# Attention and a two-layer network on one core: how Q, K and V are brought on chip

## The chip, the cores and the metric

The kernel runs on one core of a Trainium2 chip. The time is the device time of one execution in microseconds (us), lower is better. Inputs and outputs lie in the chip's memory (DRAM) as 32-bit floats; the kernel computes in bf16 with 32-bit accumulation.

## The reference, cut to what matters

```python
# q, k, v: [8 batches, 8 heads, 576 rows, 64]; beacon_k, beacon_v: [8, 8, 16, 64]
k_all = concatenate([beacon_k, k], axis=2)
v_all = concatenate([beacon_v, v], axis=2)
scores = q @ k_all.T / 8            # causal mask on the 576 own rows, beacons always seen
a = softmax(scores)
x = (a @ v_all)                     # to [4608 tokens, 512]
h = x @ w_in                        # w_in [512, 2048]
out = maximum(0.01 * h, h) @ w_out  # w_out [2048, 512]
```

## The kernel before

The attention is done in 32 steps `g`, one for each pair of heads: `g = 4 * b + hp` for batch `b` and pair `hp`. A step of the main loop does several things at once, one step apart from each other:

- `t_q(g+1, 0)` and `t_q(g+1, 1)` turn the next pair's queries and keys by TensorE (PE) transposes into `qT` and `kT`, with a copy out of PSUM by VectorE (DVE). Each takes six transposes, since the 576 rows of a head lie as 96 partitions with six rows each (`RI = 6`, `RP = 96`). The 16 beacon columns of `kT` are two small copies by GpSimd (POOL).
- `score(g, 0..3)` multiplies keys by queries; ScalarE (ACT) takes the exponential of each part into `aT`. `masks(g)` zeroes the causal triangle on DVE.
- `value(g-1, 0)` and `value(g-1, 1)` multiply `aT` by `v_aug`, whose 65th column of ones yields the row sums; DVE divides. `x_transposes(g-1)` brings the result into `xT`.
- `fill(m, n)` with `m = g - 5` puts pieces of the two-layer network (`moe1`, `moe2`) between these. So no piece of the network runs before step 5, and `w_out` is first needed in step 9. After step 32 only network pieces are left.

The order of the instructions on each engine is that of the code; nothing reorders them. Queries and keys come as plain 32-bit transfers on SyncE's queue (SP), in runs of 1536 bytes, and are cast to bf16 by POOL (the first few by DVE). Values come by POOL's own queue, whose transfers cast on the way, straight into `v_aug`; their runs in DRAM are one row, 256 bytes. The weights come by POOL's queue too, in eight transfers of 1 MB read each, runs of 2048 bytes, two of them issued in each of the first steps. POOL therefore casts queries and keys, copies beacon columns and issues transfers, all in one line.

A transfer that POOL issues takes one of eight counters in turn (`DMASW0` to `DMASW7` in the order below), so it is issued only when the transfer eight before it has landed. SP and ACT have eight of their own (`DMAHW0` to `DMAHW7`).

Of the kernel before, what the change touches and what calls it, by code (L numbers as in the profile page):

```python
# [8 lines left out]
FP32 = mybir.dt.float32  # L9
BF16 = mybir.dt.bfloat16  # L10
# [5 lines left out]
def kernel(  # L16
# [11 lines left out]
    nc = tc.nc  # L28
# [12 lines left out]
    RI = 6  # L41
    RP = S // RI

# [25 lines left out]
    natpool = ctx.enter_context(tc.tile_pool(name="natpool", bufs=2))  # L69
# [29 lines left out]
    bkT = singles.tile([128, B, H, NB], BF16, name="bkT")  # L99
# [17 lines left out]
    def load_qk(b, h0, nh, q_eng, k_eng):  # L117

        if b not in nat:
            nat[b] = (  # L120
                natpool.tile([RP, RI, H, D], BF16, name="q_nat"),
                natpool.tile([RP, RI, H, D], BF16, name="k_nat"),
            )
        hs = slice(h0, h0 + nh)
        for src, dst, name, eng in ((q, nat[b][0], "q_raw", q_eng), (k, nat[b][1], "k_raw", k_eng)):
            raw = rawpool.tile([RP, 4, RI, D], FP32, name=name)
            nc.sync.dma_start(
                out=raw[:, 0:nh],
                in_=src[b, hs].rearrange("h (p i) d -> p h i d", i=RI),
            )  # L130
            eng.tensor_copy(  # L131
                out=dst[:, :, hs, :],
                in_=raw[:, 0:nh].rearrange("p h i d -> p i h d"),
            )
# [4 lines left out]
    def load_beacon_k():  # L139
        nc.scalar.dma_start(out=bk_raw, in_=beacon_k.rearrange("b h n d -> (h n) b d"))  # L140
        nc.gpsimd.tensor_copy(
            out=bk, in_=bk_raw[:, :, None, :].to_broadcast([128, B, 2, D])
        )

    def beacon_transposes(b0, b1):

        ps = ps_one.tile([128, 1024], BF16, name="tp", tag="one")
        for b in range(b0, b1):
            nc.tensor.transpose(
                ps[:, b * 128 : (b + 1) * 128], bk[:, b].rearrange("p e d -> p (e d)"), ident  # L150
            )
        nc.vector.tensor_copy(
            out=bkT[:, b0:b1].rearrange("p b h n -> p (b h n)"), in_=ps[:, b0 * 128 : b1 * 128]
        )

    def load_v(b):
        t = v_bufs[b % 2]
        nc.gpsimd.dma_start(
            out=t[0:NB, 0, :, 0:D], in_=beacon_v[b].rearrange("h p d -> p h d")
        )  # L160
        nc.gpsimd.dma_start(
            out=t[NB:128, 0, :, 0:D], in_=v[b, :, 0:112].rearrange("h p d -> p h d")
        )
        for c in (1, 2, 3):
            nc.gpsimd.dma_start(  # L165
                out=t[:, c, :, 0:D],
                in_=v[b, :, OFF[c] : OFF[c] + 128].rearrange("h p d -> p h d"),
            )
        nc.gpsimd.dma_start(
            out=t[0:80, 4, :, 0:D], in_=v[b, :, 496:576].rearrange("h p d -> p h d")  # L170
        )
# [3 lines left out]
    def t_q(g, which):  # L175

        b, hp = divmod(g, NPAIR)
        hs = slice(2 * hp, 2 * hp + 2)
        if which == 0:
            dst = headpool.tile([128, S], BF16, name="qT")  # L180
            qk[g] = [dst]
        else:
            kT = headpool.tile([128, NB + S], BF16, name="kT")
            for par in range(2):
                ps_ = slice(par * 64, par * 64 + 64)
                nc.gpsimd.tensor_copy(out=kT[ps_, 0:NB], in_=bkT[ps_, b, 2 * hp + par, :])  # L186
            qk[g].append(kT)
            dst = kT[:, NB : NB + S]
        ps = ps_one.tile([128, 1024], BF16, name="tp", tag="one")
        for i in range(RI):  # L190
            nc.tensor.transpose(  # L191
                ps[:, i * RP : (i + 1) * RP],
                nat[b][which][:, i, hs, :].rearrange("p h d -> p (h d)"),
                ident[0:RP, 0:RP],
            )
# [161 lines left out]
    def has(g):  # L357
        return 0 <= g < NG
# [10 lines left out]
    with order:  # L369
        load_qk(0, 0, 2, nc.vector, nc.vector)  # L370
        load_beacon_k()
        load_qk(0, 2, 2, nc.vector, nc.gpsimd)
        load_v(0)
        load_qk(0, 4, 4, nc.gpsimd, nc.gpsimd)
        weights = [(load_w_in, i) for i in range(4)] + [(load_w_out, i) for i in range(4)]
        for f, i in weights[:2]:
            f(i)
        weights = weights[2:]
        beacon_transposes(0, 1)
        t_q(0, 0)  # L380
        t_q(0, 1)
        beacon_transposes(1, B)

        for g in range(NG + 1):
            b, hp = divmod(g, NPAIR)
            m = g - NPAIR - 1
            if b + 1 < B:
# [6 lines left out]
            for f, i in weights[:2]:  # L394
                f(i)
            weights = weights[2:]
# [59 lines left out]
```

## Time and profile before

| | us |
|---|---|
| median of 3 runs (lowest, highest) | 399.04 (398.98, 399.43) |
| the profiled execution | 399.55 |
| its span in the trace | 397.9 |
| PE busy in the span | 353.9 (89%) |
| ACT, DVE, POOL busy | 191.2, 168.7, 103.5 |
| bytes that the transfers wrote | 38.09 MB |

The span runs from the first to the last instruction of the trace; the 1.65 us between it and the profiled execution's time lie around it. A busy PE is not always a PE at its peak, since its instructions overlap. The transfers are counted by the bytes written, so one that casts from 32 to 16 bits counts half of what it reads. A "packet" is one run, counted on the engine that moves it; 16 transfer engines share the work, and their shares can add up to more than 1 since packets overlap. Queue q0 is POOL's, q1 is SP's, and q10 is ACT's, which brings `bk_raw` alone (1024 runs of 256 bytes, without a cast).

### The profile page before, as it was taken

Reading aid. Unit: us, or ns where it says so; the run is one execution under the profiler, and the core shown is the slowest. Engines: PE = TensorE matmul, PEld = TensorE weight load, DVE = VectorE, ACT = ScalarE, POOL = GpSimd, SP = SyncE. Lnnn points to the kernel's source line nnn. Section 1 sums busy time; section 2 is a strip of 40 time slices with the busy share of each in tenths; the row PEclk is TensorE's granted clock in tenths of the full one; section 3 lists DMA queues with packets and bytes.
Section 4 is the critical chain, followed back from the end, with each engine's and each line's share of the span. In section 5 each row is a group of like instructions: output and inputs, shape, how many; then the busy total and the mean of one; then the engine's idle time right before and its main releaser. Section 6 shows DMA issues by size and latency. Waiting matters only on the chain.

```text
span 397.9 us, 7236 instructions
## 1 busy us (share of the span) xinstructions
PE 353.9 (89%) x2997; PEld 185.0 (47%) x3048; DVE 168.7 (42%) x362; ACT 191.2 (48%) x305; POOL 103.5 (26%) x161
## 2 busy tenths in 40 slices
PE   2167068999999999999999999999999999999996
PEld 2035035565555555545555555555555454444442
DVE  3146036775445644565455445544444320101021
ACT  1063037786555555555555555555555633333300
POOL 3973375335002270237023602260000000000000
PEclk9999999999999999999999999999999999999999
DMA  8999999909005590559066905690000010100112
GB/s 203 214 226 269 209 185 217 65 2 63 28 28 145 147 89 27 147 147 87 28 147 147 88 28 147 147 87 28 28 26 28 28 54 28 53 26 28 53 54 79
DMA packets 61969, 38.09 MB, mean 96 GB/s; under 512 B 40944, under 2 KB 57328, under 8 KB 61936
## 3 DMA queue, kind: packets, MB, share of 16 engines
q0 software_dynamic: 42880, 9.05, 30.9%
q1 hardware_dynamic: 18016, 28.32, 26.8%
q8 instruction: 24, 0.39, 0.4%
q10 hardware_dynamic: 1040, 0.26, 0.3%
q14 instruction: 9, 0.07, 0.1%
HBM read 37.22 MB, written 9.44 MB: 117 GB/s over the span
## 4 chain that ended last, share of the span: by engine, by line
PE 79%; DMA 9%; DVE 3%; POOL 3%; issue 2%; ACT 2%; SPq 0%; POOLq 0%
PE acc L315 31%; PE acc L331 30%; PE av L279 7%; PE sc L214 7%; DMA w_out_sb<-in_moe_w_out_dram 5%; DMA k_raw<-in_k_dram 4%; PE tp L191 3%; ACT aT L225 2%; PE tp L301 2%; DVE aT L238 1%; POOL k_nat L131 1%; POOL v_aug L165 1%; DVE x_nat L289 1%; DVE aT L251 0%; DVE xT L306 0%
## 5 line engine op out<-in xcount | busy, mean ns | idle before, releaser
L315 PE MATMUL acc<-xT,w_in_sb 128*128 128x512 bf16 x558 | 147.5, 380 | 1.9 <-DVE xT L306 0.7
L322 ACT ACTIVATE gT<-acc 128x512 bf16<-128x512 f32 x144 | 86.3, 599 | 116.0 <-PE acc L315 114.8
L331 PE MATMUL acc<-w_out_sb,gT 128*128 128x512 bf16 x543 | 139.7, 379 | 1.6 <-DVE osb L340 0.2
L225 ACT ACTIVATE aT<-sc 128x928 bf16<-128x928 f32 (+2 forms) x128 | 102.3, 858 | 72.1 <-PE sc L214 72.1
L315 PEld LDWEIGHTS <-w_in_sb 128*128 128x128 bf16 x576 | 50.2, 97 | 62.7 <-issue 10.9
L331 PEld LDWEIGHTS <-gT 128*128 128x128 bf16 x576 | 50.9, 98 | 46.3 <-issue 0.3
L288 DVE RECIPROCAL rec<-av 128x6 f32<-128x6 f32 x64 | 12.1, 189 | 125.9 <-PE av L279 125.9
L214 PE MATMUL sc<-qT,kT 64*128 64x128 bf16 (+5 forms) x384 | 41.2, 312 | 24.6 <-POOL kT L186 22.4
L340 DVE COPY osb<-acc 128x512 f32<-128x512 f32 x36 | 24.8, 690 | 69.3 <-PE acc L331 66.9
L279 PEld LDWEIGHTS <-aT 128*128 128x128 bf16 (+1 forms) x960 | 39.9, 101 | 20.3 <-issue 5.5
L131 POOL CAST q_nat<-q_raw 96x1536 bf16<-96x1536 f32 x15 | 22.0, 1464 | 105.2 <-DMA q_raw<-in_q_dram 104.9
L279 PE MATMUL av<-v_aug,aT 128*128 128x65 bf16 (+1 forms) x960 | 43.0, 200 | 2.9 <-DMA v_aug<-in_v_dram 2.9
L214 PEld LDWEIGHTS <-kT 64*128 64x128 bf16 (+1 forms) x384 | 14.4, 100 | 50.2 <-issue 23.7
L289 DVE TENSOR_TENSOR x_nat<-av,rec 128x384 bf16<-128x384 f32 x64 | 31.4, 491 | 2.2
L186 POOL COPY kT<-bkT 64x16 bf16<-64x16 bf16 x64 | 12.6, 197 | 56.1 <-issue 42.6
L131 POOL CAST k_nat<-k_raw 96x1536 bf16<-96x1536 f32 (+1 forms) x16 | 23.9, 1491 | 8.2 <-DMA k_raw<-in_k_dram 7.2
L196 DVE COPY kT<-tp 128x576 bf16<-128x576 bf16 x32 | 24.1, 753 | 2.4 <-PE sc L214 0.5
L196 DVE COPY qT<-tp 128x576 bf16<-128x576 bf16 x32 | 23.9, 745 | 0.0
L165 POOL DMA_DIRECT2D v_aug<-in_v_dram x24 | 21.2, 901 | 9.3 <-DMA w_in_sb<-in_moe_w_in_dram 9.3
L238 DVE TENSOR_TENSOR aT<-aT,mask 128x224 bf16<-128x224 bf16 x32 | 16.1, 502 | 9.6 <-ACT aT L225 9.6
L245 DVE TENSOR_TENSOR aT<-aT,mask 128x768 bf16<-128x768 bf16 x32 | 18.9, 590 | 0.8 <-ACT aT L225 0.8
L306 DVE COPY xT<-tp 128x576 bf16<-128x576 bf16 x32 | 14.5, 453 | 9.9 <-PE tp L301 9.8
(29 smaller groups left out, 139.3 us busy)
## 6 DMA issues: line engine op xcount, KB each, us to landing
out_dram<-osb SPq DMA_DIRECT2D x36, 256.0 KB, 2.1
q_raw<-in_q_dram SPq DMA_DIRECT2D x15, 576.0 KB, 6.0
k_raw<-in_k_dram SPq DMA_DIRECT2D x15, 576.0 KB, 7.2
v_aug<-in_v_dram POOLq DMA_DIRECT2D x24, 128.0 KB, 5.5
w_in_sb<-in_moe_w_in_dram POOLq DMA_DIRECT2D x4, 512.0 KB, 21.9
w_out_sb<-in_moe_w_out_dram POOLq DMA_DIRECT2D x4, 512.0 KB, 15.6
v_aug<-in_v_dram POOLq DMA_DIRECT2D x8, 112.0 KB, 4.0
v_aug<-in_v_dram POOLq DMA_DIRECT2D x8, 80.0 KB, 5.4
```

The source lines that it names most:

```text
L131: eng.tensor_copy(out=dst[:, :, hs, :], in_=raw[:, 0:nh].rearrange("p h i d -> p i h d"),)
L165: nc.gpsimd.dma_start(out=t[:, c, :, 0:D], in_=v[b, :, OFF[c] : OFF[c] + 128].rearrange("h p d -> p h d"),)
L196: nc.vector.tensor_copy(out=dst.rearrange("c (p i) -> c p i", i=RI), in_=ps[:, 0:S].rearrange("c (i p) -> c p i", i=RI),)
L214: nc.tensor.matmul(out=sc[0 : ROWS[c], par, col - c0 : col - c0 + w], lhsT=kT[ps_, c * 128 : c * 128 + ROWS[c]], rhs=qT[ps_, q0 : q0 + w], ...
L225: nc.scalar.activation(out=aT[:, :, c0 : c0 + w], in_=sc[:, :, 0:w], func=AF.Exp, scale=0.125)
L238: nc.vector.tensor_tensor(out=aT[:, :, 0:112], in0=aT[:, :, 0:112], in1=tri[:, None, 16:128].to_broadcast([128, 2, 112]), op=ALU.mult,)
L279: nc.tensor.matmul(out=avv[:, n, 0 : D + 1], lhsT=aT[0 : ROWS[c], par, a0 : a0 + 128], rhs=va[0 : ROWS[c], c, 2 * hp + par, :], start=(c = ...
L289: nc.vector.tensor_tensor(out=x_nat[:, t0:t1].rearrange("p t e d -> p (t e) d"), in0=avv[:, :, 0:D], in1=rec[:, n0:n1, None].to_broadcast( ...
L315: nc.tensor.matmul(out=acc, lhsT=w_in_sb[:, j, fc * 128 : (fc + 1) * 128], rhs=xT[:, j, i * 512 : (i + 1) * 512], start=(j == 0), stop=(j ...
L322: nc.scalar.activation(out=gT[i][:, fc, :], in_=acc, func=AF.Prelu, alpha=0.01)
L331: nc.tensor.matmul(out=acc, lhsT=gT[i][:, fc, t * 128 : (t + 1) * 128], rhs=w_out_sb[:, fc, :], start=(fc == 0), stop=(fc == NF - 1),)
L340: nc.vector.tensor_copy(out=osb, in_=acc)
```

## The change

- Queries and keys: `load_qk(b, grp)` brings four heads in four transfers on POOL's queue, which cast on the way, with nine rows (2304 bytes) to a run. Heads 0 and 1 of the group go to partitions 0 to 63, heads 2 and 3 to partitions 64 to 127. `permute_qk` then reorders bf16 to bf16, on DVE for batch 0 and on POOL after.
- `t_q` takes nine transposes of 64 partitions instead of six of 96, from the lower or the upper half of the partitions. The beacon columns of `kT` are one copy by DVE.
- Values: `load_v` uses SP's queue without a cast, into `v_raw`, and `cast_v` makes `v_aug` from it, on DVE for batch 0 and on POOL after.
- Order: all of `w_in` is issued after batch 0's queries and keys, batch 1's queries and keys after it in step 0, and `w_out` in step 2. In a step, `t_q(g+1, 0)` now stands directly ahead of `score(g, 0)` and `t_q(g+1, 1)` directly ahead of `score(g, 2)`; the network pieces 0 to 3 stand between.

```diff
-    RI = 6
+    RI = 9
...
+    def load_qk(b, grp):
...
+        for e in range(2):
+            h0 = 4 * grp + 2 * e
+            for src, dst in zip((q, k), qk_raw[b, grp]):
+                nc.gpsimd.dma_start(
+                    out=dst[e * RP : (e + 1) * RP],
+                    in_=src[b, h0 : h0 + 2].rearrange("h (p i) d -> p h i d", i=RI),
+                )
...
+    def permute_qk(b, grp, q_eng, k_eng):
...
+        for eng, src, dst in zip((q_eng, k_eng), qk_raw.pop((b, grp)), nat[b, grp]):
+            eng.tensor_copy(out=dst, in_=src.rearrange("p h i d -> p i h d"))
...
     def load_v(b):
+        t = rawpool.tile([128, NKB, H, D], FP32, name="v_raw")
+        v_raws[b] = t
+        nc.sync.dma_start(out=t[0:NB, 0], in_=beacon_v[b].rearrange("h p d -> p h d"))
+        nc.sync.dma_start(out=t[NB:128, 0], in_=v[b, :, 0:112].rearrange("h p d -> p h d"))
+        for c in (1, 2, 3, 4):
+            nc.sync.dma_start(
...
+    def cast_v(b, eng):
+        t, dst = v_raws.pop(b), v_bufs[b % 2]
+        for c in range(NKB):
+            eng.tensor_copy(out=dst[0 : ROWS[c], c, :, 0:D], in_=t[0 : ROWS[c], c])
...
-            for par in range(2):
-                ps_ = slice(par * 64, par * 64 + 64)
-                nc.gpsimd.tensor_copy(out=kT[ps_, 0:NB], in_=bkT[ps_, b, 2 * hp + par, :])
+            nc.vector.tensor_copy(out=kT[:, 0:NB], in_=bkT[:, b, hp])
...
+            if g == 0:
+                load_qk(1, 0)
+                load_qk(1, 1)
+            elif g == 2:
+                for i in range(4):
+                    load_w_out(i)
+            if g == 0:
+                permute_qk(0, 1, nc.vector, nc.vector)
             if b + 1 < B:
                 if hp == 0:
-                    load_qk(b + 1, 0, 4, nc.gpsimd, nc.gpsimd)
-                elif hp == 1:
-                    load_qk(b + 1, 4, 4, nc.gpsimd, nc.gpsimd)
-                elif hp == 2:
                     load_v(b + 1)
...
+                if hp >= 2:
+                    permute_qk(b + 1, hp - 2, nc.gpsimd, nc.gpsimd)
+                if b >= 1 and hp < 2:
+                    load_qk(b + 1, hp)
+                if hp == 3:
+                    cast_v(b + 1, nc.gpsimd)
             if has(g + 1):
                 t_q(g + 1, 0)
-            fill(m, 0)
-            if has(g + 1):
-                t_q(g + 1, 1)
-            fill(m, 1)
             if has(g):
                 score(g, 0)
                 score(g, 1)
-            fill(m, 2)
+            if g == 0:
+                cast_v(0, nc.vector)
+            fill(m, 0)
+            fill(m, 1)
             if has(g - 1):
                 value(g - 1, 0)
+            fill(m, 2)
             fill(m, 3)
+            if has(g + 1):
+                t_q(g + 1, 1)
```

On POOL, from the last weights of step 2 to the beacon columns of steps 3 and 4, these rows stand before the change (what an instruction waits for is in brackets; `PE_49`, `DVE_49` and the like are the engines' own counters):

```order
L111 DMA w_out_sb<-in_moe_w_out_dram 128x4x512 [waits DMASW3_49]
L186 COPY kT<-bkT 64x16 [waits DVE_49,PE_49]
L186 COPY kT<-bkT 64x16 [waits Pool_49]
L158 DMA v_aug_93<-in_beacon_v_dram 16x8x64 [waits DMASW4_49]
L161 DMA v_aug_93<-in_v_dram 112x8x64 [waits DMASW5_49]
L165 DMA v_aug_93<-in_v_dram 128x8x64 [waits DMASW6_49]
L165 DMA v_aug_93<-in_v_dram 128x8x64 [waits DMASW7_49]
L165 DMA v_aug_93<-in_v_dram 128x8x64 [waits DMASW0_49]
L169 DMA v_aug_93<-in_v_dram 80x8x64 [waits DMASW1_49]
L111 DMA w_out_sb<-in_moe_w_out_dram 128x4x512 [waits DMASW2_49]
L111 DMA w_out_sb<-in_moe_w_out_dram 128x4x512 [waits DMASW3_49]
L186 COPY kT<-bkT 64x16 [waits DVE_49,PE_49]
```

In the changed kernel, POOL has this at the same place, from the end of batch 1's first loads in step 0 to the values of batch 1 in step 3:

```order
L130 DMA k_raw<-in_k_dram 64x2x576 [waits DMASW7_49]
L130 DMA q_raw<-in_q_dram 64x2x576 [waits DMASW0_49,DVE_49]
L130 DMA k_raw<-in_k_dram 64x2x576 [waits DMASW1_49,DVE_49]
L130 DMA q_raw<-in_q_dram 64x2x576 [waits DMASW2_49]
L130 DMA k_raw<-in_k_dram 64x2x576 [waits DMASW3_49]
L112 DMA w_out_sb<-in_moe_w_out_dram 128x4x512 [waits DMASW4_49]
L112 DMA w_out_sb<-in_moe_w_out_dram 128x4x512 [waits DMASW5_49]
L112 DMA w_out_sb<-in_moe_w_out_dram 128x4x512 [waits DMASW6_49]
L112 DMA w_out_sb<-in_moe_w_out_dram 128x4x512 [waits DMASW7_49]
L142 COPY q_nat<-q_raw 128x1152
L142 COPY k_nat<-k_raw 128x1152
L142 COPY q_nat<-q_raw 128x1152 [waits DMASW2_49,DMASW0_49,PE_49]
```

The beacon copies have left POOL; the two reorderings of batch 1's first half (`L142`, `q_nat` and `k_nat`) now stand behind all four transfers of `w_out`, the last of which waits for the fourth transfer of that half.

On DVE, in step 0 between the keys of pair 0 and the masks, the changed kernel has this, where before there were only the copies of `qT` and `kT`:

```order
L208 COPY kT<-tp 128x576 [waits PE_49]
L142 COPY q_nat<-q_raw 128x1152 [waits DMASW6_49,DMASW4_49]
L142 COPY k_nat<-k_raw 128x1152 [waits DMASW7_49,DMASW5_49]
L208 COPY qT<-tp 128x576 [waits PE_49]
L184 CAST v_aug_92<-v_raw 128x8x64 [waits DMAHW2_49,DMAHW0_49]
L184 CAST v_aug_92<-v_raw 128x8x64 [waits DMAHW3_49]
L184 CAST v_aug_92<-v_raw 128x8x64 [waits DMAHW4_49]
L184 CAST v_aug_92<-v_raw 128x8x64 [waits DMAHW5_49]
L184 CAST v_aug_92<-v_raw 80x8x64 [waits DMAHW6_49]
L198 COPY kT<-bkT 128x16
L208 COPY kT<-tp 128x576 [waits PE_49]
```

The keys of pair 1 (the last row) now stand behind the reordering of batch 0's second half and behind the cast of all of batch 0's values.

## Rows read from the trace of the kernel before

**Rows 1.** The page's span in 40 slices: busy tenths of PE and of the transfer engines.
```profile
PE   2167068999999999999999999999999999999996
...
DMA  8999999909005590559066905690000010100112
```

**Rows 2.** Busy time by stretch (us, count): PE, PEld, DVE, ACT, POOL; PEclk, DMA share, GB/s.
```profile
0.00:2.00 2.00, 0.00 (x0) 0.00 (x0) 0.20 (x1) 1.19 (x1) 1.32 (x9) 1.00 0.06 13
...
39.20:52.60 13.40, 0.27 (x4) 0.06 (x1) 1.40 (x3) 0.00 (x0) 4.17 (x6) 1.00 1.64 198
...
90.70:325.00 234.30, 231.48 (x2110) 120.43 (x2147) 117.74 (x259) 132.43 (x212) 54.84 (x87) 1.00 0.45 80
```

**Rows 3.** Waits from 0 to 64 us: total us, times, longest.
```profile
PE sc L214 <- POOL kT L186: 22.4, 3, 13.2
```

**Rows 4.** POOL in order of time: start us, us, instruction, count, idle before.
```profile
9.51 0.66 POOL L158 DMA_DIRECT2D v_aug<-in_beacon_v_dram  x1
...
51.60 0.74 POOL L111 DMA_DIRECT2D w_out_sb<-in_moe_w_out_dram  x1 [2.03 <-DMA w_out_sb<-in_moe_w_out_dram]
52.38 0.94 POOL L186 COPY kT<-bkT 64x16 bf16<-64x16 bf16 x4
```

**Rows 5.** PE in order of time, steps 2, 3 and the start of 5.
```profile
32.15 0.69 PE L191 MATMUL tp<-ident,q_nat 96*128 96x96 bf16 x6
32.64 0.68 PE L191 MATMUL tp<-ident,k_nat 96*128 96x96 bf16 x6
33.25 0.99 PE L214 MATMUL sc<-qT,kT 64*128 64x512 bf16 x4
34.17 0.84 PE L279 MATMUL av<-v_aug,aT 128*128 128x65 bf16 x12
...
38.30 0.69 PE L191 MATMUL tp<-ident,q_nat 96*128 96x96 bf16 x6
...
63.78 0.42 PE L191 MATMUL tp<-ident,q_nat 96*128 96x96 bf16 x6
```

**Rows 6.** PE in order of time, a later step, with the network between.
```profile
189.82 0.42 PE L191 MATMUL tp<-ident,q_nat 96*128 96x96 bf16 x6
190.08 1.03 PE L315 MATMUL acc<-xT,w_in_sb 128*128 128x512 bf16 x4
...
193.55 0.53 PE L279 MATMUL av<-v_aug,aT 128*128 128x65 bf16 x12
193.92 0.38 PE L331 MATMUL acc<-w_out_sb,gT 128*128 128x512 bf16 x1
```

**Rows 7.** Transfer queues (packets, MB written, share), stretches 5:8, 43:48, 18:20, 3:4.
```profile
q1 hardware_dynamic: 526, 0.74, 109.5%
...
q0 software_dynamic: 1039, 1.03, 124.2%
...
q0 software_dynamic: 2383, 0.30, 277.0%
...
q10 hardware_dynamic: 952, 0.24, 105.8%
```

**Rows 8.** The same for 22:27 (both queues) and 10:15 (SP's alone).
```profile
q1 hardware_dynamic: 745, 1.10, 95.9%
q0 software_dynamic: 748, 0.10, 29.5%
...
q1 hardware_dynamic: 802, 1.18, 109.6%
```

**Rows 9.** Instructions by line and shape: busy us, mean ns, idle before.
```profile
L196 DVE COPY qT<-tp 128x576 bf16<-128x576 bf16 x32 | 23.9, 745 | 0.0
L131 POOL CAST q_nat<-q_raw 96x1536 bf16<-96x1536 f32 x15 | 22.0, 1464 | 105.2 <-DMA q_raw<-in_q_dram 104.9
L191 PEld LDWEIGHTS <-q_nat 96*128 96x128 bf16 x192 | 12.6, 105 | 5.3 <-issue 0.2
L131 DVE CAST q_nat<-q_raw 96x768 bf16<-96x768 f32 x2 | 1.1, 556 | 3.3 <-DMA q_raw<-in_q_dram 3.3
```

More of the change, by code (lines that the diff above doesn't have):

```diff
@@ L115 @@
     nat = {}
[L117 to L134, printed above, removed]
+    qk_raw = {}
+    def load_qk(b, grp):
+        qk_raw[b, grp] = (
+            rawpool.tile([128, 2, RI, D], BF16, name="q_raw"),
+            rawpool.tile([128, 2, RI, D], BF16, name="k_raw"),
+        )
[5 more added lines that the diff above has]
+                    in_=src[b, h0 : h0 + 2].rearrange("h (p i) d -> p h i d", i=RI),
+                )
+    def permute_qk(b, grp, q_eng, k_eng):
+        nat[b, grp] = (
+            natpool.tile([128, RI, 2, D], BF16, name="q_nat"),
+            natpool.tile([128, RI, 2, D], BF16, name="k_nat"),
+        )
+        for eng, src, dst in zip((q_eng, k_eng), qk_raw.pop((b, grp)), nat[b, grp]):
+            eng.tensor_copy(out=dst, in_=src.rearrange("p h i d -> p i h d"))
     bk_raw = singles.tile([128, B, D], FP32, name="bk_raw")
@@ L151, in beacon_transposes @@
             )
-        nc.vector.tensor_copy(
-            out=bkT[:, b0:b1].rearrange("p b h n -> p (b h n)"), in_=ps[:, b0 * 128 : b1 * 128]
-        )
-    def load_v(b):
[L157 to L167, printed above, removed]
-            )
-        nc.gpsimd.dma_start(
-            out=t[0:80, 4, :, 0:D], in_=v[b, :, 496:576].rearrange("h p d -> p h d")
-        )
+        for par in range(2):
+            ps_ = slice(par * 64, par * 64 + 64)
+            nc.vector.tensor_copy(
+                out=bkT[ps_, b0:b1].rearrange("p b h n -> p (b h) n"),
+                in_=ps[ps_, b0 * 128 : b1 * 128].rearrange("p (x e n) -> p e x n", e=2, n=NB)[:, par],
+            )
+    v_raws = {}
+    def load_v(b):
+        t = rawpool.tile([128, NKB, H, D], FP32, name="v_raw")
[4 more added lines that the diff above has]
+            nc.sync.dma_start(
+                out=t[0 : ROWS[c], c],
+                in_=v[b, :, OFF[c] : OFF[c] + ROWS[c]].rearrange("h p d -> p h d"),
+            )
+    def cast_v(b, eng):
+        t, dst = v_raws.pop(b), v_bufs[b % 2]
+        for c in range(NKB):
+            eng.tensor_copy(out=dst[0 : ROWS[c], c, :, 0:D], in_=t[0 : ROWS[c], c])
     qk = {}
@@ L177, in t_q @@
         b, hp = divmod(g, NPAIR)
-        hs = slice(2 * hp, 2 * hp + 2)
+        grp, e = divmod(hp, 2)
+        ps_ = slice(e * RP, (e + 1) * RP)
         if which == 0:
@@ L192, in t_q @@
                 ps[:, i * RP : (i + 1) * RP],
[L193 to L194 removed]
+                nat[b, grp][which][ps_, i].rearrange("p h d -> p (h d)"),
+                ident[ps_, ps_],
             )
@@ L369 @@
     with order:
-        load_qk(0, 0, 2, nc.vector, nc.vector)
         load_beacon_k()
-        load_qk(0, 2, 2, nc.vector, nc.gpsimd)
+        load_qk(0, 0)
         load_v(0)
[L374 to L379, printed above, removed]
+        load_qk(0, 1)
+        for i in range(4):
+            load_w_in(i)
+        permute_qk(0, 0, nc.vector, nc.vector)
+        beacon_transposes(0, B)
         t_q(0, 0)
         t_q(0, 1)
-        beacon_transposes(1, B)
         for g in range(NG + 1):
```

11 lines of the change are left out of this document (5 added, 6 removed).

## The prediction

> **What bounds it now.** Read the span in slices first [rows 1]: from the eighth slice on PE is at nine tenths, and before that it has holes, the largest in the fifth, while the transfer engines are full for the first seven. Then the stretches [rows 2]: from 90.7 to 325 PE is busy 231.5 of 234.3 us, so nothing but less PE work could shorten that; from 39.2 to 52.6 it is busy 0.27 of 13.4 us. The waits say for what [rows 3]: 22.4 us for POOL's beacon copy of `kT`, 13.2 at once. POOL in order of time shows why the copy is late [rows 4]: it stands behind value and weight transfers, each of which waits for the transfer eight before it; the last is issued at 51.6 and the copies run at 52.38. So the start is bound by how fast the transfers drain and by what stands behind them on POOL. Step 5, the first with network work, begins with its transposes at 63.78 [rows 5]. All later time is PE's, so the sum is simple: when does step 5 begin now, and does a later step cost PE more?
>
> **Prices of the transfers** [rows 7]. A plain 1536-byte run: 526 in 3 us, 175 per us. A cast weight run of 2048 bytes: 1039 in 5 us, 77 ns on one of 16 engines, so 512 runs (one transfer) take 2.46 us and `w_in` 9.9. A cast 256-byte run: 2383 in 2 us. A plain 256-byte run: 952 in 1 us, 17 ns on an engine. A batch of values has 16x8 + 112x8 + 3x128x8 + 80x8 = 4736 runs, 296 an engine: 4.0 us before, 5.0 now, so the values' move gains nothing in the transfers themselves. A cast run of 2304 bytes is not there. By the weight run's time per byte it takes 77 x 2304/2048 = 87 ns, by the plain query run's 91 x 2304/1536 = 137 ns. I take 87: same queue, same cast, nearly the same length. Four heads of queries and keys (512 runs, 32 an engine) then take 2.8 us (4.4 at the other end); before, 768 plain runs took 4.4.
>
> **How two queues share.** The rows show two things [rows 8]. Once both have work they go one for one (745 and 748 packets in 5 us). But POOL's values, issued from 9.51 on [rows 4], moved nothing at first: SP's queue alone filled 10 to 15 us. Now SP holds the values (plain) and POOL the queries, keys and weights, so I work out both ends. The Trainium skill (DMA: Bandwidth & Descriptors, Queues, rings and completion order) says that each transfer engine goes round robin between its queues packet by packet. By that alone end B below would hold; the first stretch does not agree with it, the second does.
>
> *End A: POOL's queue starts when batch 0's values are through.* Transfers start at about 2 us [rows 2]; ACT's beacons (1024 runs) take 1.1, values 5.0: 8.1. From then one for one with batch 1's values: a pair costs 87 + 17 = 104 ns beside queries and keys, 77 + 17 = 94 beside weights. Batch 0's first half is there at 8.1 + 32 x 0.104 + about 1 to land = 12.4, its second half at 15.8. `w_in` (128 an engine, 12.0) ends at 26.8, batch 1's first half at 30.1, landed 31. POOL must then issue the last `w_out` (0.75 [rows 4]) and reorder twice, 1152 elements at the pace of its casts (1464 ns for 1536 [rows 9]): 1.1 each. `t_q(4, 0)` of step 3 can run at 34.0.
> On DVE (a 768-element cast is 556 ns, a PSUM copy 745 [rows 9]) batch 0's second half is reordered at 17.0, `qT` 17.7, five value casts at about 0.4 to 19.7, `kT` 20.6; so step 1's scores start at 20.6.
>
> *End B: one for one from 4 us on.* Batch 0's values have 48 of 296 turns behind them; 248 more run beside queries and keys (64 x 0.104), `w_in` (128 x 0.094) and 56 x 0.104 of batch 1: they end at 28.5, land at 29. DVE stands at its value cast until then; `kT` follows at 30.3. Batch 1's first half is there by then.
>
> **What a step of the start costs.** Step 2 before ran from 32.15 to 38.30, 6.15 us [rows 5], with no stall for transfers. In it 0.61 us pass between the key transposes (32.64) and the scores (33.25). They move into the time in which PE waits for the exponentials, so I take 5.5 (6.15 if nothing is hidden; 4.5 if the faster pace of PE comes earlier: twelve 65-column products take 0.84 us here [rows 5] and 0.53 later [rows 6], though the granted clock reads 1.00 in all of it).
> End A: step 2 at 20.6 - 0.6 + 5.5 = 25.5, step 3 at 31.0, waits until 34.0, step 4 at 39.5, step 5 at 45.0. End B: step 2 at 35.2, step 5 at 51.7. I take the middle, 48.4: 15.4 us earlier than 63.78.
> What is late next: batch 1's values (592 turns from the start) end at about 38 to 44 in either end, cast by POOL in 2.5, needed by step 5 at 48. Batch 2's first half stands behind `w_out` (128 x 94 ns) and lands at about 50 to 54, is reordered by 57, and is needed by step 7, two steps of some 6.5 us after 48.4: 61. Covered, by 4 us.
>
> **What a later step costs.** Per `t_q`, six transposes of 96 columns took 0.26 us (189.82 to 190.08 [rows 6]); nine of 64 at the pace of the 65-column products (12 in 0.37, so 31 ns) are 0.28. 52 of the 64 lie after step 5: +1.0 us. The beacon copies move to DVE, which is half idle there (117.7 of 234.3 [rows 2]), POOL's casts become smaller reorderings and POOL is busy 54.8: nothing. The order of the pieces within a step changes no sum while PE never waits; its cover is PE's queue itself.
>
> Sum against the profiled execution: 399.55 - 15.4 + 1.0 = 385.1. The runs' median lies 0.5 under that execution: **384.6**. Its own range, with ends A and B and 0.6 us a step either way, is 380 to 389.
>
> **Rivals.**
> *The start is no longer bound by transfers* (376): steps 1 to 4 run on from 20.6 at 5.5 or less, step 5 at about 40, 23 us earlier. For it: nothing needed by step 3 costs more than 31 us. Against: batch 1 stands behind all of `w_in`, and the two reorderings behind `w_out`.
> *Values or queries late* (392): at 137 ns a run, five halves add 5 x 1.6 = 8 us ahead of batch 2, three of them (4.8) ahead of step 3; or end B with steps of 6.15, step 5 at 54.3. Gain 5 to 9. For it: one-for-one turns punish short runs, and DVE's whole line waits for batch 0's values. Against: batch 0's values start first.
> *The stall only moves* (399): step 3 waits for POOL again. It takes a landing of batch 1 at about 49 instead of 31; only a queue that stands still for some 18 us would do that, which no row shows.
> *Slower: transposes with bare weight loads* (420). All nine transposes of a `t_q` use the same half of the array's rows. If a weight load could not run under the transpose before it, each would cost 105 ns [rows 9] + 29, nine 1.2 us, 0.94 more than now; 52 of them 49 us, and at half a load 23. It decides from 0.28 us more a `t_q`, where 52 of them eat the 14.4 us of gain. Against: 12 products in 0.37 us load 12 full weights under each other. The Trainium skill (TensorE: Matmul & The Clock Gate, Part 3: Packing small matmuls — row/col tiling) says that a weight load overlaps with running products only where the row groups differ. By that this rival holds; the 31 ns a product do not agree, but they are for all 128 rows, and no row here has short products on one half.
>
> **Chances.** The forecast 0.54, no bound at the start 0.13, late 0.20, only moved 0.04, slower 0.09. A change of 0.2% (0.8 us) is about what a measurement tells here: faster 0.87, same 0.04, slower 0.09. The range takes in the first three cases: 375 to 394.
>
> **What would show it.** Right: step 5's first network product at about 48 us; no wait for a copy of `kT` on POOL; a query run at 85 to 95 ns on an engine; a later step still at 9.8 us (234.3 over 24 steps [rows 2]). Wrong: a later step above 10.2 us (transposes), DVE idle for `v_raw` at 20 to 30 us (end B or worse), POOL's reordering before step 3 or 7 later than PE's need, or the q0 queue idle while SP's values run beyond 8 us.

## The result, and the profile after

The changed kernel takes 382.16 us (median of 4 runs, 381.69 to 384.12), the kernel before 399.01 beside it (398.65 to 399.43): a ratio of 0.9587, with a 95% interval of 0.9558 to 0.9617. The profiled execution is the slowest of the four, 384.12 us with a span of 382.3. Of the executions behind the medians of the experiments, those over 1.5% above the fastest of the same kernel are left out: one each in experiment 5 (its profiled one, 1996 us), in both forms of experiment 6 and in the first form of experiment 7 (its profiled one, 414.71 us).

The page's slices of after (busy tenths of TensorE, its granted clock, the transfer engines) stand against [rows 1]:

```profile
PE   1464999999999999999999999999999999999995
...
PEclk9998579999999999999999999999999999999999
DMA  9999999836077107720664043000000000101012
```

TensorE's hole in the fifth slice is gone, and from the fifth slice on it reads nine. A new mark is in the clock: the fourth to sixth slice read 8, 5, 7. What TensorE and VectorE still wait for in the first 64 us (total us, times, longest), against [rows 3]:

```profile
PE sc L226 <- DVE kT L208: 6.2, 2, 4.8
...
PE tp L203 <- DVE q_nat L142: 5.3, 1, 5.3
...
DVE v_aug L184 <- DMA v_raw<-in_v_dram: 3.7, 1, 3.7
PE av L291 <- DVE aT L250: 3.6, 1, 3.6
...
PE tp L203 <- POOL q_nat L142: 0.9, 1, 0.9
```

The 22.4 us for GpSimd's beacon copies are no longer there. TensorE in order of time, the start of steps 3, 4, 5 and 9 and one later step, against [rows 5, 6]:

```profile
33.76 0.37 PE L203 MATMUL tp<-ident,q_nat 64*128 64x64 bf16 x7 [0.90 <-POOL q_nat L142]
...
42.82 0.50 PE L203 MATMUL tp<-ident,q_nat 64*128 64x64 bf16 x6
...
48.49 0.55 PE L203 MATMUL tp<-ident,q_nat 64*128 64x64 bf16 x7
...
75.47 0.38 PE L203 MATMUL tp<-ident,q_nat 64*128 64x64 bf16 x7
...
173.23 1.03 PE L343 MATMUL acc<-w_out_sb,gT 128*128 128x512 bf16 x4
174.19 0.38 PE L203 MATMUL tp<-ident,q_nat 64*128 64x64 bf16 x7
174.39 0.39 PE L226 MATMUL sc<-qT,kT 64*128 64x512 bf16 x1
174.41 0.22 PE L203 MATMUL tp<-ident,q_nat 64*128 64x64 bf16 x2
174.47 0.57 PE L226 MATMUL sc<-qT,kT 64*128 64x512 bf16 x3
174.97 1.04 PE L327 MATMUL acc<-xT,w_in_sb 128*128 128x512 bf16 x4
```

Step 5 begins at 48.49 instead of 63.78, 15.3 us earlier; that is nearly the whole difference of the two spans (397.9 - 382.3 = 15.6). Step 9 begins at 75.47, where before it began at 90.52. The next step after the one shown begins at 183.99, so a later step lasts 9.80 us, as before.

On the way to step 5 there is something that no row of before had shown at this size. VectorE in order of time:

```profile
21.08 0.42 DVE L184 CAST v_aug<-v_raw 80x512 bf16<-80x512 f32 x1 [3.69 <-DMA v_raw<-in_v_dram]
...
32.43 5.76 DVE L250 TENSOR_TENSOR aT<-aT,mask 128x224 bf16<-128x224 bf16 x1
```

And GpSimd at the same time:

```profile
32.52 1.18 POOL L142 COPY q_nat<-q_raw 128x1152 bf16<-128x1152 bf16 x1
...
35.78 1.17 POOL L142 COPY k_nat<-k_raw 128x1152 bf16<-128x1152 bf16 x1
36.87 1.19 POOL L184 CAST v_aug<-v_raw 128x512 bf16<-128x512 f32 x2
```

A mask that takes 0.27 us at the median of the 32 steps took 5.76, and it ended 0.13 us after GpSimd's run of six operations (32.43 + 5.76 = 38.19 against 36.87 + 1.19 = 38.06). Smaller cases could have been read in the trace of before, VectorE:

```profile
76.86 1.51 DVE L238 TENSOR_TENSOR aT<-aT,mask 128x224 bf16<-128x224 bf16 x1
```

It ended at 78.37, 0.13 us after the one cast of GpSimd beside it (76.78 to 78.24). In after, TensorE stood 3.65 us for the mask, and then worked at a low granted clock. Busy time by stretch (columns as in [rows 2]; PEclk is the third number from the end):

```profile
38.25:48.50 10.25, 9.27 (x118) 6.57 (x118) 8.30 (x23) 5.08 (x8) 0.62 (x1) 0.50 1.22 202
74.40:309.00 234.60, 234.12 (x2289) 122.23 (x2288) 117.72 (x284) 133.18 (x213) 56.18 (x77) 1.00 0.33 70
```

The two transfer queues from 20 to 21 us (packets, MB written, share):

```profile
q0 software_dynamic: 154, 0.16, 91.9%
q1 hardware_dynamic: 159, 0.04, 29.8%
```

They go one for one, some 154 pairs in 1 us, 104 ns of one transfer engine for a pair. GpSimd's packets write 0.16 MB, 1024 bytes each, so these are weight runs.

### The profile page after: what moved, and what is told of

Read it like the earlier page. It is cut to its first block, busy times and chain, and to the rows that moved or that the text cites. A ratio compares the mean times of both kernels' runs of the same rounds, so it can differ in the third digit from the quotient of the medians.

```text
span 382.3 us, 7642 instructions
## 1 busy us (share of the span) xinstructions
PE 354.7 (93%) x3240; PEld 185.1 (48%) x3240; DVE 174.0 (46%) x401; ACT 192.3 (50%) x305; POOL 98.0 (26%) x144
## 4 chain that ended last, share of the span: by engine, by line
PE 90%; DMA 4%; DVE 3%; SPq 1%; issue 0%; DVEq 0%
PE acc L327 34%; PE acc L343 33%; PE av L291 9%; PE sc L226 7%; PE tp L203 5%; DMA v_raw<-in_v_dram 4%; PE tp L313 2%; DVE aT L250 2%; SPq L176 1%; DVE x_nat L301 1%; DVE aT L257 0%; DVE rec L300 0%; DVE osb L352 0%; DVE kT L208 0%; SPq L174 0%
## 5 line engine op out<-in xcount | busy, mean ns | idle before, releaser
L343 PE MATMUL acc<-w_out_sb,gT 128*128 128x512 bf16 x576 | 145.2, 379 | 0.0
L343 PEld LDWEIGHTS <-gT 128*128 128x128 bf16 x576 | 53.6, 98 | 57.4 <-issue 0.8
L226 PE MATMUL sc<-qT,kT 64*128 64x208 bf16 (+5 forms) x384 | 44.7, 311 | 6.7 <-DVE kT L208 6.2
L300 DVE RECIPROCAL rec<-av 128x6 f32<-128x6 f32 x64 | 12.1, 189 | 80.8 <-PE av L291 80.8
L142 POOL COPY q_nat<-q_raw 128x1152 bf16<-128x1152 bf16 x14 | 16.4, 1172 | 77.4 <-PE tp L203 68.5
L184 POOL CAST v_aug<-v_raw 128x512 bf16<-128x512 f32 (+1 forms) x35 | 20.6, 617 | 16.5 <-DMA v_raw<-in_v_dram 11.8
L226 PEld LDWEIGHTS <-kT 64*128 64x128 bf16 (+1 forms) x384 | 20.4, 101 | 8.9 <-DVE kT L208 6.5
L142 POOL COPY k_nat<-k_raw 128x1152 bf16<-128x1152 bf16 x14 | 16.2, 1158 | 26.7 <-PE tp L203 26.7
L130 POOL DMA_DIRECT2D k_raw<-in_k_dram x32 | 20.6, 644 | 6.2 <-DMA w_in_sb<-in_moe_w_in_dram 5.7
L130 POOL DMA_DIRECT2D q_raw<-in_q_dram x32 | 20.1, 628 | 5.7 <-DMA w_in_sb<-in_moe_w_in_dram 5.4
L203 PE MATMUL tp<-ident,q_nat 64*128 64x64 bf16 x288 | 15.2, 200 | 6.2 <-DVE q_nat L142 5.3
L318 DVE COPY xT<-tp 128x576 bf16<-128x576 bf16 x32 | 14.5, 454 | 11.6 <-PE tp L313 11.1
```

Of the source, the lines that this page charges most:

```text
L130: nc.gpsimd.dma_start(out=dst[e * RP : (e + 1) * RP], in_=src[b, h0 : h0 + 2].rearrange("h (p i) d -> p h i d", i=RI),)
L142: eng.tensor_copy(out=dst, in_=src.rearrange("p h i d -> p i h d"))
L203: nc.tensor.transpose(ps[:, i * RP : (i + 1) * RP], nat[b, grp][which][ps_, i].rearrange("p h d -> p (h d)"), ident[ps_, ps_],)
L226: nc.tensor.matmul(out=sc[0 : ROWS[c], par, col - c0 : col - c0 + w], lhsT=kT[ps_, c * 128 : c * 128 + ROWS[c]], rhs=qT[ps_, q0 : q0 + w], ...
L343: nc.tensor.matmul(out=acc, lhsT=gT[i][:, fc, t * 128 : (t + 1) * 128], rhs=w_out_sb[:, fc, :], start=(fc == 0), stop=(fc == NF - 1),)
```

## The experiments

Every ratio is to the kernel before, run beside it on the same chip (400.2 us in the first four, 399.8 to 400.4 in the others), with its 95% interval.

**1. The kernel before, with one line of the change: the beacon copies of `kT` on VectorE.**

```
-                nc.gpsimd.tensor_copy(out=kT[ps_, 0:NB], in_=bkT[ps_, b, 2 * hp + par, :])
+                nc.vector.tensor_copy(out=kT[ps_, 0:NB], in_=bkT[ps_, b, 2 * hp + par, :])
```

> The kernel before with one part of the change alone: the beacon columns of kT are copied by DVE instead of POOL (the same two small copies); all loads, formats and casts stay as before. Theory A (the 13.2 us stall was POOL's line, not the amount to be transferred): step 3's scores start at about 40 instead of 52.6, steps 3 and 4 take about 6 us each, and step 5 then waits for the casts of batch 1's second half, which stand on POOL behind w_out (at 53.4 in the profile before, queries ready at 54.9): step 5 at about 55 instead of 63.8, the time about 390 (388 to 392). Theory B (the new transfer formats make the start shorter): the beacon copy is only the last in line and step 3 starts near 52 all the same, 397 to 399.5.

387.26 us, ratio 0.969 (0.9652 to 0.9727): 3.1 of the 4.1 per cent come from this line alone. Theory A holds, but step 5 begins 8 us earlier than I had expected and the time is below my range. Its start, TensorE in order of time:

```profile
47.14 0.69 PE L191 MATMUL tp<-ident,q_nat 96*128 96x96 bf16 x6
...
52.89 0.25 PE L279 MATMUL av<-v_aug,aT 128*128 128x65 bf16 x3 [1.20 <-DMA v_aug<-in_v_dram]
```

Step 5 begins even earlier than in after, at 47.14. TensorE still waits for values that stand behind other transfers, 9.7 us in eight pieces, of which three lie behind the start of step 5 (2.6 us), and step 9 begins at 78.00 against 75.47 in after. So the other edits together are worth the rest, some 4 us by the two ratios; step 9 accounts for 2.5 of it. Which of the new loads does it was not tested one by one, except for the values (experiment 6).

**2. After, with the old order of the pieces within a step.**

```
+            fill(m, 0)
+            if has(g + 1):
+                t_q(g + 1, 1)
+            fill(m, 1)
             if has(g):
                 score(g, 0)
                 score(g, 1)
```

(and these three taken out where the change had put them, `fill(m, 2)` ahead of the first value product.)

> The changed kernel with the old order within a step (both t_q first, with network piece 0 between them, then piece 1, the scores, pieces 2 and 3 around the first half of the values, as before the change); loads as in the changed kernel. Theory A (PE never waits in a later step, so order there is worth nothing; at the start the keys' transposes are hidden by the exponentials only in the new order): steps 2 and 4 about 0.6 us longer each, step 1 and 3 hidden by other waits: 383 to 384.5 against 382.2. Rival (the new order itself keeps PE fed, nine short transposes need the scores beside them): each later step longer by 0.1 us or more, over 385.

395.31 us, ratio 0.9885 (0.9844 to 0.9926). The expectation was 11 to 12 us off, and with it fell my sentence that the order costs nothing. Step 5 begins at 47.36, so it isn't the start. A later step lasts 10.23 us instead of 9.80, and its rows show where:

```profile
179.73 0.43 PE L203 MATMUL tp<-ident,q_nat 64*128 64x64 bf16 x9
180.09 1.04 PE L327 MATMUL acc<-xT,w_in_sb 128*128 128x512 bf16 x4
181.06 0.43 PE L203 MATMUL tp<-ident,k_nat 64*128 64x64 bf16 x9
181.43 1.04 PE L343 MATMUL acc<-w_out_sb,gT 128*128 128x512 bf16 x4
182.40 0.59 PE L226 MATMUL sc<-qT,kT 64*128 64x512 bf16 x4
```

From start to start, the network piece at 180.09 takes 0.97 us where its successor has 64 rows of weights; a network piece followed by products of 128 rows takes 0.87 (174.97 to 175.84 in after). The transposes take 0.36 instead of 0.27, since 128 rows follow them. Each border between products of 64 and of 128 rows costs 0.1 us, and the old order has four more of them in a step than the new one, where `t_q` stands right beside the scores, which are 64 rows too. From the start of step 9 to that of step 30 the 0.43 us a step make 9.0 us (215.56 us against 206.61 in after). Steps 6 to 8, with no piece of the second layer yet, take 6.85 us instead of 6.35, and step 5 began 1.1 us earlier. The spans differ by 10.6 us (392.9 - 382.3), the medians by ratio by 11.6 (395.31 against 0.9587 x 400.22 = 383.7). The price could have been read ahead of time, since the scores of before have such borders. TensorE in before, just behind [rows 6]:

```profile
190.94 0.42 PE L191 MATMUL tp<-ident,k_nat 96*128 96x96 bf16 x6
191.20 1.03 PE L331 MATMUL acc<-w_out_sb,gT 128*128 128x512 bf16 x3
192.16 0.58 PE L214 MATMUL sc<-qT,kT 64*128 64x512 bf16 x4
```

The network piece ahead of the scores takes 0.96 us (191.20 to 192.16; one of its four records is missing), the one ahead of 96-row transposes 0.86 (190.08 to 190.94). The weight loads show what differs. The load ahead of 96-row transposes in before, and the one ahead of 64-row transposes here:

```profile
190.73 0.49 PEld L191 LDWEIGHTS <-k_nat 96*128 96x128 bf16 x6
```

```profile
181.06 0.31 PEld L203 LDWEIGHTS <-k_nat 64*128 64x128 bf16 x9 [0.42 <-issue]
```

The first runs 0.21 us ahead of its transposes (190.94), under the piece before them; the second starts with its transposes (181.06), after 0.42 us without a load. One load's record lasts some 0.1 us (95 ns at the median in after). So the first load behind a border isn't covered. Whether the 0.1 us are this load or something that ends ahead of it, no run here tells apart.

**3. After, with batch 1's reorderings on VectorE, in steps 3 and 4.**

```
+            if g in (3, 4):
+                permute_qk(1, g - 3, nc.vector, nc.vector)
...
-                if hp >= 2:
+                if hp >= 2 and b >= 1:
                     permute_qk(b + 1, hp - 2, nc.gpsimd, nc.gpsimd)
```

> The changed kernel with the reordering of batch 1's two halves on DVE (first half at the start of step 3, second half at the start of step 4) instead of back to back on POOL in steps 2 and 3; all else the same. In the profile of the changed kernel DVE's mask of step 2 lasts from 32.43 to 38.19, as long as POOL's run of four reorderings and two casts, and PE waits 3.65 us for it. Theory A (DVE's masks cannot run beside POOL's copies, which follow each other without a gap): the mask takes under 2 us, the wait of 3.65 us is gone, two queries' reorderings of 0.75 us come onto PE's path instead: step 5 at 45 to 47 instead of 48.5, and PE is not left idle for 4 us, so its granted clock need not fall: 377 to 380.5. Rival (the mask is late for another reason, a semaphore that POOL's other work sends): the long mask stays, 382 to 384.

381.27 us, ratio 0.9532 (0.9505 to 0.9558): 0.2% below after by the medians, 0.6% by the ratios, whose intervals meet. The trace says more than the time. The same mask on VectorE:

```profile
33.33 0.61 DVE L250 TENSOR_TENSOR aT<-aT,mask 128x224 bf16<-128x224 bf16 x1
```

With GpSimd's four reorderings gone it takes 0.61 us, beside one cast of GpSimd, so it was that run that held it. Step 5 begins at 46.00: 2.5 us, not the 3.65 of the wait, since the queries of group 4 now wait 1.94 us for VectorE.

**4. After, with the casts of batch 0's values behind `kT(1)` on VectorE.**

```
-            if g == 0:
-                cast_v(0, nc.vector)
             fill(m, 0)
...
                 t_q(g + 1, 1)
+            if g == 0:
+                cast_v(0, nc.vector)
```

> The changed kernel with the cast of batch 0's values moved behind the copy of pair 1's keys on DVE (in step 0 it stood ahead of it). In the profile of the changed kernel step 1's scores wait 4.8 us for those keys, since DVE stands at the cast of the last 80 rows until 21.1. Theory A (two limits in a row: step 3 must wait for batch 1's reordering at 33.8 in any case, where only 0.9 us of waiting were left): step 1's scores start at about 18 instead of 22.3, but the values of step 0 still wait until 22, and what is won is lost again at step 3, whose wait grows to 2 or 3 us: 381 to 382.5, within 0.3% of the changed kernel. Rival (the 4.8 us are on the path to the end): 377 to 379.

380.70 us, ratio 0.9515 (0.9491 to 0.9538): more than expected. TensorE and then VectorE:

```profile
33.67 0.55 PE L203 MATMUL tp<-ident,q_nat 64*128 64x64 bf16 x7 [2.17 <-POOL q_nat L142]
...
44.86 0.37 PE L203 MATMUL tp<-ident,q_nat 64*128 64x64 bf16 x7
```

```profile
31.07 0.27 DVE L250 TENSOR_TENSOR aT<-aT,mask 128x224 bf16<-128x224 bf16 x1
```

As expected, step 3 begins no earlier (33.67 against 33.76): it waits for GpSimd's reordering. Not expected: because step 2 ran earlier, its masks were through at 32.0 us, before GpSimd's run began at 32.46, and step 5 comes 3.6 us earlier. This is the same 5.76 us mask again, avoided by another edit.

**5. After, with batch 1's queries and keys ahead of `w_in` 1 to 3,** and their reorderings ahead of GpSimd's issue of `w_out`.

```
-        for i in range(4):
-            load_w_in(i)
+        load_w_in(0)
+        load_qk(1, 0)
+        load_qk(1, 1)
+        for i in range(1, 4):
+            load_w_in(i)
```

> After's order of loads with batch 1's queries and keys ahead of the input weights 1 to 3, and their reorderings ahead of the issue of the output weights. Theory A (step 3 waited because batch 1's first half stood behind three weight blocks that nothing needs before step 6): the queries of group 4 wait for nothing, step 5 begins at 44.5 to 46.5 us instead of 48.5 and the time is 379.5 to 381 us (ratio to before 0.950 to 0.955). Rival B (what is gained there is lost again, because GpSimd's reorderings now lie beside another mask, or because the values of batch 1 come later still): step 5 at 48 to 49 and the time within 0.3% of after (ratio 0.956 to 0.961).

381.68 us, ratio 0.953 (0.9489 to 0.9572), which reaches into both expectations. It was run for a trace again:

> The kernel with batch 1's queries and keys ahead of the input weights 1 to 3 once more, for a trace: the profiled execution of its first run took 1994 us, with TensorE at a fraction of its pace from start to end, while its timed runs took 380.6 to 382.2. Theory A: the queries of group 4 wait for nothing and step 5 begins at 44.5 to 46.5 us. Rival B: step 5 at 48 to 49, since GpSimd's reorderings lie beside a mask again.

380.62 us in that one execution. TensorE, the starts of steps 5 and 9:

```profile
45.23 0.37 PE L203 MATMUL tp<-ident,q_nat 64*128 64x64 bf16 x7
...
72.62 0.38 PE L203 MATMUL tp<-ident,q_nat 64*128 64x64 bf16 x7
```

Theory A holds: the queries of group 4 wait for nothing, and 2.9 us are left at step 9. The stall moved in part. Step 1's scores now wait 7.1 us for `kT`, whose copy stands behind the last value cast on VectorE, and that cast is stretched too:

```profile
21.58 2.73 DVE L184 CAST v_aug<-v_raw 80x512 bf16<-80x512 f32 x1 [3.53 <-DMA v_raw<-in_v_dram]
```

It takes 0.42 us in after; here two reorderings of GpSimd lie beside it (21.79 to 24.03).

**6. After, with V by casting transfers on GpSimd's queue again.**

```
-        t = rawpool.tile([128, NKB, H, D], FP32, name="v_raw")
+        t = v_bufs[b % 2]
...
-            nc.sync.dma_start(
-                out=t[0 : ROWS[c], c],
+            nc.gpsimd.dma_start(
+                out=t[0 : ROWS[c], c, :, 0:D],
```

> After, with only the move of V undone: the values come by casting transfers on GpSimd's queue as before, in the place that the program gives them, and no engine casts them. Theory A (two queues that share the transfer engines one for one let 4736 packets of 256 B delay the 2 KB packets; one queue in order is quicker for what is needed first): the values of batch 0 have landed by 16 us, batch 1's first half by 29, step 5 begins at 43 to 46 and the time is 378 to 381 us (ratio 0.947 to 0.955). Rival B (the values ahead in the same queue and their six issues of 0.9 us on GpSimd delay queries, keys and weights by more than sharing did): step 5 at 49 to 52, 383 to 386 us (ratio 0.959 to 0.967).

The first form was flawed: it loaded the values of batch b+1, from b = 1 on, over those of batch b-1 while one value product of these was still ahead, which changes that product and makes TensorE wait (up to 6.0 us). Its 408.65 us (1.0218) aren't the edit's. Mended:

> After with only the move of V undone, mended in the same way (values of batch b+1 loaded two steps later for b of 1 and above; without that the value products waited for them). Theory A (a casting transfer of the values costs the same machine time as the shared plain one, some 5 us a batch, so the move gains nothing in transfers; what it moves is who waits): GpSimd's issues of the values (five of 0.84 to 0.9 us) stand ahead of its reorderings of batch 1, the queries of group 4 wait 6 to 9 us for these, step 5 begins at 48 to 51 and the time is 381.5 to 385 us (ratio 0.955 to 0.964). Rival B (moving V freed the casting queue and is worth several us): step 5 at 53 or later, above 387 us (ratio above 0.968).

383.23 us, ratio 0.9561 (0.9503 to 0.9618): no different from after. TensorE:

```profile
37.55 0.55 PE L201 MATMUL tp<-ident,q_nat 64*128 64x64 bf16 x7 [6.67 <-POOL q_nat L142]
...
48.35 0.38 PE L201 MATMUL tp<-ident,q_nat 64*128 64x64 bf16 x7
```

Theory A holds in mechanism and size: step 5 begins at 48.35 against 48.49. Alone in the casting queue a batch of values passes in about 5 us; as plain runs they hold the other queue at 154 weight runs of 2 KB per us instead of some 205 (18 to 24 us here), and for longer. What is gained in one place (no cast on VectorE, no 3.69 us for `v_raw`) is lost in the other (6.67 us for a reordering that GpSimd does behind six more issues).

**7. Everything in one queue in the order of need:** queries and keys 0a, values 0, queries and keys 0b and 1a, `w_in` 0, queries and keys 1b, values 1, the other weights; batch 1's reorderings on VectorE in steps 2 and 4.

```
+        load_qk(1, 0)
+        load_w_in(0)
+        load_qk(1, 1)
+        load_v(1)
+        for i in range(1, 4):
+            load_w_in(i)
...
+            if g in (2, 4):
+                permute_qk(1, g // 2 - 1, nc.vector, nc.vector)
```

> After with all of it in one queue in the order of need (queries and keys 0a, values 0, queries and keys 0b and 1a, input weights 0, queries and keys 1b, values 1, the other weights), values cast in the transfer, and batch 1's reorderings on VectorE in steps 2 and 4. Theory A (steps 0 to 4 are bound by what lands when, so that each of these waits can be taken out): step 5 begins at 37 to 41 us, later steps stay at 9.8 us, and the time is 370 to 375 us (ratio 0.927 to 0.939). Rival B (with the waits gone the five steps are bound by TensorE's own half pace before the granted clock rises, or by VectorE's copies): step 5 at 43 to 45 and 377 to 379 us (ratio 0.944 to 0.949).

The same flaw as in experiment 6 gave 405.97 us (1.0159); its trace has a wait of 17.1 us in step 4, which began at 34.47. Mended, and with values 0 behind queries and keys 0b:

> The run in the order of need again, with its flaw mended: there the values of batch b+1 (b of 1 and above) were loaded in the step in which the last value product of batch b-1's buffer still stood ahead, so the products waited up to 17 us for them; now they are loaded two steps later, as before the change. Besides, the values of batch 0 stand behind queries and keys 0b instead of ahead of them. Up to step 4 the flaw did nothing: that step began at 34.5 us, with 2.4 us of wait for the queries of 0b. Theory A (only landing times held steps 0 to 4): step 5 begins at 37 to 39.5 us, a later step stays at 9.8, and the time is 372.5 to 375.5 us (ratio to before 0.931 to 0.941). Rival B (GpSimd's long list of issues, which waits for transfers to end before it can give more, now makes the values of batch 1 or the later reorderings late): step 5 at 37 to 40 too, but waits of over 2 us after it and 377 to 380 us (ratio 0.944 to 0.952).

381.33 us, ratio 0.9522 (0.9489 to 0.9555). TensorE:

```profile
36.39 0.55 PE L201 MATMUL tp<-ident,q_nat 64*128 64x64 bf16 x7
...
57.38 0.55 PE L201 MATMUL tp<-ident,q_nat 64*128 64x64 bf16 x7 [6.83 <-POOL q_nat L142]
...
66.46 0.35 PE L201 MATMUL tp<-ident,q_nat 64*128 64x64 bf16 x6
...
72.81 0.38 PE L201 MATMUL tp<-ident,q_nat 64*128 64x64 bf16 x7
```

Step 5 came 12 us earlier than in after, and step 9 only 2.7: theory B. Batch 2's queries stood behind all the weights, and their reordering behind GpSimd's issues of batch 2's values, and behind the wait of 6.83 us TensorE was busy all the time at a low clock:

```profile
57.40:62.50 5.10, 5.10 (x33) 2.29 (x33) 1.64 (x4) 2.46 (x3) 5.10 (x7) 0.50 1.58 51
```

So the step that begins at 57.38 takes 9.08 us with TensorE never waiting, the next one 6.35. The time is even above B's range, since I had counted the wait alone: 6.8 us of wait and 2.7 of slower pace.

**8. Experiment 1, with the new order of the pieces within a step as well.**

```
             if has(g + 1):
                 t_q(g + 1, 0)
+            if has(g):
+                score(g, 0)
+                score(g, 1)
             fill(m, 0)
-            if has(g + 1):
-                t_q(g + 1, 1)
             fill(m, 1)
```

> The kernel before with the beacon copies on VectorE (the first of these experiments) and, besides, the new order of pieces within a step; loads and six transposes of 96 rows as before. Theory A (a product of 64 rows of weights beside one of 128 rows costs 0.1 us at each border; 96-row transposes pay no such border, and the scores paid theirs already): a later step keeps its 9.8 us, and the time is that of the first experiment within 0.5% (ratio 0.965 to 0.974). Rival B (any run of transposes between two network products costs it, and the new order is worth the 11 us by itself): a later step at 9.4 us, 374 to 378 us (ratio 0.937 to 0.947).

388.11 us, ratio 0.9701 (0.9665 to 0.9736), the same as experiment 1 within the intervals. The same point of two later steps that follow each other, on TensorE:

```profile
173.69 0.42 PE L191 MATMUL tp<-ident,k_nat 96*128 96x96 bf16 x6
...
183.49 0.42 PE L191 MATMUL tp<-ident,k_nat 96*128 96x96 bf16 x6
```

9.80 us, so theory A holds. In a later step the new order is worth nothing by itself; it is what keeps the 64-row transposes from costing some 10 us. In steps 6 to 8, where TensorE still waits a little in experiment 1 (busy 19.26 of 19.92 us), it is worth 0.29 us each (6.35 against 6.64). The whole times don't show that, since here step 5 takes 15.57 us instead of 10.94 and step 9 begins at 80.75 instead of 78.00.

**9. Experiment 7 mended, carried on to batch 2:** its first half ahead of `w_out`, its second half behind it, both reordered by VectorE.

```
             if g == 2:
+                load_qk(2, 0)
                 for i in range(4):
                     load_w_out(i)
+                load_qk(2, 1)
...
-            if g in (2, 4):
-                permute_qk(1, g // 2 - 1, nc.vector, nc.vector)
+            if g in (2, 4, 6, 8):
+                permute_qk(1 + g // 6, (g // 2 - 1) % 2, nc.vector, nc.vector)
```

> The order of need carried on to batch 2: in the run before, step 5 began at 36.4 us as expected, and then step 7 stood 6.8 us for batch 2's queries, which GpSimd had reordered at 56.1, behind its issues of batch 2's values and behind the output weights in its queue. Here batch 2's first half is issued ahead of the output weights and its second half right behind them, and VectorE reorders both, in steps 6 and 8. Theory A (what was gained at step 5 was given back there and nowhere else): step 5 begins at 36 to 37 us, step 7 waits for nothing, step 9 begins at 62.5 to 64 us instead of 72.8, and the time is 370.5 to 373.5 us (ratio to before 0.927 to 0.936). Rival B (the casting queue, which moves some 205 runs of 2 KB per us and is full from 5 to 60 us, is now itself the bound: output weights or values of batch 2 come late for step 9): waits of 2 to 6 us by step 9, 374 to 378 us (ratio 0.936 to 0.947).

371.25 us, ratio 0.9261 (0.9223 to 0.93): theory A, and faster than both kernels. TensorE:

```profile
36.27 0.38 PE L201 MATMUL tp<-ident,q_nat 64*128 64x64 bf16 x7
...
63.28 0.38 PE L201 MATMUL tp<-ident,q_nat 64*128 64x64 bf16 x7
```

Step 9 begins at 63.28, 12.2 us earlier than in after; the medians differ by 10.9 (382.16 - 371.25). From 75 to 305 us TensorE is busy 230.00 of 230.00 us. Of the other 140 us it is idle for 14.5 ahead of step 5, 0.6 from there to 75 and 4.0 behind 305, so nearly all that is left to gain outside of its own work lies ahead of step 5.

## Why the prediction was right, point by point

*The bound.* Right, and the largest part: GpSimd's beacon copy behind its transfers. Experiment 1 takes out that alone and gets three quarters of the gain.

*The start, 48.4.* It came at 48.49, but not by the way that the prediction took: that is luck. Step 1's scores ran at 22.30 (A 20.6, B 30.3) and step 3 at 33.76 (A 34.0). These are nearly A's times, but not A's transfers: batch 0's values weren't through at 8.1, and VectorE stood 3.69 us for their last part, until 21.08. From 33.76 two steps at my 5.5 us give 44.8. The rest is the blocked mask, which I hadn't seen: without its 3.65 us step 3 took 5.41 (42.82 - 33.76 - 3.65), and step 4 took 5.67. The half clock behind it is not a part of this difference, since my 5.5 was read from rows of that pace. Experiments 3 and 4 take the mask's stall away by different edits and begin step 5 at 46.00 and 44.86. The middle of two ends hit because an unknown cost of their half distance came in.

*Sharing and prices.* Both pairs cost more than I took. Beside weights I had 94 ns, and 104 was measured (20 to 21 us). Beside queries and keys I had 104: from 27 to 33 us 924 packets went against 927, but they wrote 0.94 MB, so some 816 of them were runs of 1152 bytes written, which is 118 ns a run. Alone in its queue a query run takes 91 ns (0.61 MB, so some 530 runs, from 27 to 30 us in experiment 6), near my 87, so a pair costs more than the two prices that I added. SP's values moved mostly first, though not alone as in end A (3032 packets against 687 of the other queue from 3 to 10 us), and then the queues went one for one, as in end B (1595 against 1570 from 10 to 20). That the move of the values gains nothing was right (experiment 6).

*Late next.* Too kind. Batch 1's values were cast by 50.3 us, not 40 to 47, and batch 2's first half was reordered by 61.7, not 57. In after nobody waited for them, but there was little to spare (step 7's transposes came at 62.76): 3.3 us earlier at step 5 cost 1.0 us for the values and 0.8 for batch 2's queries (experiment 5), and 12 us earlier cost 6.83 (experiment 7).

*A later step, +1.0.* Wrong: 9.80 against 9.80 to 9.81 before. The term stood on "The order of the pieces within a step changes no sum while PE never waits", and that is the step that failed. Nine 64-row transposes run at 28 to 30 ns each, near the 31 that I took, but they come with borders that cost 0.1 us each, which the new order removes again. The forecast of the total was within 2.5 us because two effects of some 10 us cancel, one of which I had set to nothing and the other not seen. Of the 2.4 us (384.6 against 382.16) 1.0 is this term (385.1 against 384.12 for the profiled execution), and the rest is that after's profiled execution lies 1.96 us above the median, where I had put 0.5. The rival of slower transposes (420) had the wrong mechanism, a bare weight load for each transpose, and the right suspicion: with the old order the gain falls to 4.9 us, and at each border one load isn't covered.

## What to carry to other kernels

A stall of an idle engine's tiny copy is read from the in-order line in which it stands; moving that copy can be worth more than moving megabytes. Put loads into one order by the step that first needs them and follow each wait that you remove to the next consumer, for here a gain of 12.1 us at step 5 had shrunk to 2.7 at step 9 (experiment 7) until batch 2 was moved as well (experiment 9). Before products change their number of rows, look at which neighbours they get, and price a border from starts of instructions, not from their durations.

## What the runs showed of the hardware

*Borders on TensorE.* 0.1 us for each change between products of 64 and 128 rows of weights, with TensorE never waiting (experiment 2, and 0.96 against 0.86 in before); 96 rows beside 128 pay nothing. The Trainium skill (TensorEngine Tiling (Array Packing), Key Properties) says that a change of the tiling mode drains TensorE. If a change between 64 and 128 rows is one, these rows agree and give it a price, about 0.1 us at the full clock; that it is a drain, and not the uncovered load that the rows show, is not shown.

*GpSimd holds VectorE.* A mask of 0.27 us took 5.76, as long as GpSimd worked back to back, and a cast of 0.42 took 2.73. The Trainium skill (SBUF — State Buffer, SBUF: two separate sides) says that the two engines share a pair of ports as an exclusive lock, held for the whole instruction. The rows agree that one blocks fully, and show that VectorE can be passed over: here it got no turn between six instructions of GpSimd. It isn't always so: at 62.94 in after a mask of 0.28 us took 1.23 and ended 0.15 us behind the first of GpSimd's instructions (64.02), while the next already ran. When it gets its turn stays open.

*The clock.* After the wait of 3.65 us the granted clock of the next 10 us is 0.50, the lower of the two levels, though TensorE was busy 9.27 of 10.25 us; after the wait of 6.83 us in experiment 7 it is 0.50 again, with TensorE busy throughout. So such a wait costs more than its length. How much more can be read where a step has no wait of its own: step 7 of experiment 7 took 9.08 us and step 8 6.35, which puts 2.7 us on the slower pace behind the wait. In after, step 4 took 5.67 at 0.50, and 4.54 in experiment 5 at 1.00; step 5 took 7.92, and 6.37 in experiment 6, where the clock had risen ahead of it. The page's clock reads 9 from the start of the span, but there it can't be trusted: twelve 65-column products take 0.84 us at 23.23 in after, and the same 0.84 at 44.22, where the granted clock is 0.50.
